# A recurrent-attention and MLP kernel: who issues the transfers, and a new written-out order

## The chip, the cores and the metric

The kernel runs on one core of a Trainium2 chip. A core has five engines with their own instruction queues: TensorE (PE in the profile), VectorE (DVE), ScalarE (ACT), GpSimd (POOL) and SyncE (SP), which here only issues transfers. Each queue is worked off strictly in order; an instruction that has to wait holds everything behind it on its engine. SyncE, ScalarE and GpSimd can issue DMA transfers, which sixteen DMA engines carry out. The metric is the device time of one launch in microseconds (us). Differences of less than about one per cent are hard to tell from no change.

## The reference

Two steps follow each other. The first is a recurrence over time with a per-channel decay, for 4 batches and 8 heads, 768 steps, head dimension 48:

```python
for t in range(S):
    kt, vt, rt, wt = (k[:, :, t], v[:, :, t], r[:, :, t], w[:, :, t])
    cur = np.einsum('bhd,bhe->bhde', u[None] * kt, vt)
    y[:, :, t] = np.einsum('bhd,bhde->bhe', rt, state + cur)
    state = wt[:, :, :, None] * state + np.einsum('bhd,bhe->bhde', kt, vt)
```

The second takes the result as 3072 rows of 384 numbers through an MLP with a softmax-gated activation and a normalisation:

```python
h = x @ w_in                              # 384 -> 1024
sm = softmax(h); solu = h * sm
ln = (solu - mean(solu)) / sqrt(var(solu) + 1e-6) * g_ln
out = ln @ w_out                          # 1024 -> 384
```

Inputs and outputs are float32: 18.9 MB of r, k, v and w, two weights of 1.6 MB each, 4.7 MB of output.

## The kernel before, in words

The time axis is cut into 6 chunks of 128 steps. A chunk of one batch, all 8 heads, is a unit; there are 24, numbered so that the four batches of a chunk follow each other (unit 4 is chunk 1 of batch 0). A unit is handled in matrix form. Its stages, by the names of the order:

- LW, LK, LR, LV load w, k, r, v of the unit (192 KB each, in rows of 192 bytes) into rings of 7 buffers. LU, LG, LI (three parts) and LO (two parts) load u, the gain g, w_in and w_out.
- lw takes the logarithm of w (ScalarE); cum sums it over time by two products (TensorE); ex takes exponentials in place (ScalarE); kp scales k and r by them (VectorE).
- krk and krr transpose the scaled k and r (TensorE), kr copies the result out of PSUM; M forms the scores (TensorE); m copies them, masked (VectorE, letter d) or unmasked (ScalarE, letter a), in which case sel masks them on GpSimd.
- p, q, dg, dv form the bonus term with u: p = k r, q = p u, dv = v dg on GpSimd, the row sum dg on VectorE. vb casts v.
- Y multiplies scores and v and adds the state's part; with the letter i it also adds dv by a product, otherwise y adds dv while copying on VectorE. S, et and st carry the state to the next chunk.
- X transposes y, xT copies it, H is the first MLP product (24 matmuls), e its exponential (ScalarE), he = h e (VectorE), hq its square. Oa and Ob are the two halves of the output product with the scaled weight w2, together with the sums for mean and variance. sq, qm, lv make the scale, o writes the scaled output, out stores it.
- Once per launch: wi casts w_in, gw scales w_out by g into w2 (eight pieces), mn and mc form the mean over rows of w2 and ce adds it (eight pieces: "centring"). Oa of unit 0 needs the centred pieces 0 to 3.
- us and uc spread u over the partitions by a product with a row of ones, gs and gc bring g into columns. hot issues n dummy products of 512 columns whose result is not used.

The order of all this work is written out by hand in ORDER: one word per stage, with the unit's number and, after the dot, a PSUM slot, the engine that does a copy (a ScalarE, d VectorE, p GpSimd) or, for loads, the queue that issues it (s SyncE, a ScalarE). The loop at the end of the kernel walks through the words, and the class InOrder ties each engine's instructions to that order, so no scheduler moves them. Before the loop stand the constants: masks, identities and the zero columns, on GpSimd and VectorE.

In the built program the transfers issued by SyncE and ScalarE share eight completion counters in turn. A transfer therefore waits, on its issuing engine, until the one eight places earlier in that turn has landed, besides waiting until its buffer is free.

Of the kernel before, what the change touches and what calls it, by code (L numbers as in the profile page):

```python
# [8 lines left out]
F32 = mybir.dt.float32  # L9
# [12 lines left out]
LW0.a LK0.s LU0.a LR0.s LW1.a LW2.s hot4.s3 LG0.s LK1.s lw0 LV0.a cum0.b0 LR1.s us0.s0 ex0 hot2.s3 uc0 lw1 LV1.s  # L22
p0 kp0 LW3.a LK2.a LR2.s krk0.s3 q0 krr0 cum1.b1 kr0.a hot2.s2 LV2.s LK3.a M0.b0 LR3.s p1 gs0.s1 ex1 m0.d
hot3.s3 LI1.s lw2 q1 dg0 cum2.b0 lw3 hot2.s3 kp1 vb0.p LI0.a S0.s2 dv0 vb1.a dg1 hot1.s3 ex2 Y0.is0 et0 LV3.a
cum3.b1 LI2.s p2 kp2 krk1.s3 gc0 LO0.s ex3 st0 LW4.s krk2.s1 q2 krr1 LO1.s krr2 kp3 kr1.a hot3.s2 dv1 LK4.s
kr2.d y0.a p3 M1.b0 LK5.a S1.s2 dg2 krk3.s3 vb2.a m1.d krr3 et1 wi0.a S2.s0 wi1.p M2.b1 st1 X0.s1 kr3.a m2.d
Y1.is2 LR4.s wi2.p et2 y1.a M3.b0 xT0.d LV4.a X1.s3 q3 m3.d H0.b1 dv2 gw1.a dg3 gw2.d e0 Y2.is2 LW5.s xT1.d
gw3.p st2 H1.b0 y2.a he0 lw4 gw0.a X2.s1 LR5.s e1 gw7.d cum4.b1 gw4.d hot2.s3 gw6.d gw5.d ex4 he1 vb3.p mn0.s3
LW6.s LV5.a dv3 xT2.a LK6.s kp4 S3.s0 mc0 Y3.is2 LR6.s lw5 ce6.d krk4.s1 ce3.d hq0.a cum5.b0 ce4.d krr4 ce2.d
H2.b1 ce7.d ex5 LW7.s ce1.d ce5.d ce0.d y3.a LK7.s p4 kp5 et3 Oa0.s3 lw6 e2 LR7.s kr4.d p5 krk5.s2 cum6.b0 st3  # L30
hq1.a Ob0 vb4.p he2 LW8.s q4 krr5 ex6 S4.s1 LK8.s kr5.d sq0 M4.b1 lw7 Oa1.s0 kp6 et4 m4.a LR8.s X3.s2 qm0 st4
vb5.p M5.b0 xT3.a cum7.b1 dg4 sel4 lv0 krk6.s1 LV6.s Ob1 m5.d ex7 LW9.s dv4 lw8 S5.s2 kp7 o0.a krr6 LK9.s p6
cum8.b0 sq1 et5 Y4.ns3 kr6.d ex8 H3.b1 q5 LV7.s y4.d hq2.a kp8 q6 LR9.s krk7.s1 e3 X4.s3 st5 LW10.s vb6.p M6.b0
krr7 xT4.d Oa2.s2 dg5 m6.a LK10.s qm1 kr7.d dv5 krk8.s3 lv1 Ob2 he3 out0 sel6 o1.a lw9 M7.b0 out1 dg6 S6.s1 sq2
m7.a LV8.s hq3.d krr8 cum9.b1 LR10.s Y5.ns0 vb7.p qm2 kr8.d lv2 H4.b0 p7 LW11.s et6 y5.d ex9 st6 p8 lw10 kp9
LV9.s X5.s3 S7.s0 e4 Oa3.s1 q7 o2.d vb8.a he4 out2 cum10.b1 dv6 xT5.a krk9.s2 et7 LK11.s ex10 Y6.ns3 q8 krr9 st7
LV10.s H5.b0 hq4.a kp10 sel7 LR11.s kr9.a y6.d M8.b1 dg7 LW12.s S8.s0 lw11 m8.d Ob3 dv7 et8 e5 LV11.s vb9.p
krk10.s3 st8 X6.s2 LK12.s p9 M9.b1 he5 xT6.a Y7.ns0 sq3 m9.a krr10 LR12.s S9.s2 dg8 cum11.b0 et9 LW13.s y7.d
H6.b1 lw12 dv8 ex11 kr10.d LK13.s p10 qm3 lv3 kp11 Oa4.s0 LR13.s e6 q9 st9 X7.s3 cum12.b0 LW14.s xT7.a Ob4 he6
p11 ex12 LV12.s krk11.s2 sel9 sq4 Y8.ns3 o3.a kp12 H7.b1 hq5.a out3 vb10.p qm4 y8.d q10 LK14.s lv4 dg9 M10.b0 e7  # L40
Oa5.s1 LR14.s m10.d vb11.p q11 o4.a krr11 LW15.s X8.s3 lw13 dg10 Ob5 p12 xT8.a out4 he7 kr11.a S10.s0 dv9 S11.s3
LV13.s dg11 sq5 hq6.a Y9.ns2 vb12.p qm5 cum13.b0 y9.d dv10 LK15.s H8.b1 et10 ex13 st10 LR15.s et11 lw14 kp13
Oa6.s2 LW16.s e8 hq7.d krk12.s0 lw15 M11.b0 p13 st11 LK16.s Ob6 lv5 he8 o5.a q12 krr12 m11.a Y10.ns3 out5 kr12.d
krk13.s1 cum14.b1 LR16.s y10.d sq6 krr13 sel11 ex14 cum15.b0 LW17.s kr13.d Oa7.s0 ex15 qm6 LV14.s kp14 p14
Y11.ns3 lw16 X9.s1 Ob7 kp15 lv6 dv11 LK17.s vb13.a xT9.d p15 o6.a M12.b1 y11.d M13.b0 m12.a X10.s1 out6 m13.d
krk14.s2 q13 S12.s3 LR17.s hq8.a krr14 H9.b1 dg12 LV15.s vb14.p xT10.d sq7 q14 et12 qm7 st12 LW18.s lv7 krk15.s1
dg13 e9 X11.s3 sel12 H10.b0 o7.d kr14.a out7 he9 dv12 LK18.s Y12.ns0 xT11.a p16 krr15 LR18.s Oa8.s2 e10 y12.d
kr15.d q15 LV16.s cum16.b1 he10 S13.s0 ex16 dv13 Ob8 LV17.s et13 kp16 q16 X12.s3 LW19.s Y13.ns1 sq8 xT12.a st13
M14.b0 vb15.p M15.b1 LK19.s m14.a y13.d krk16.s3 S14.s0 hq9.d krr16 LR19.s m15.a S15.s1 p17 qm8 kr16.d H11.b0
LW20.s et14 dg14 lv8 sel14 st14 et15 LK20.s dg15 H12.b1 e11 vb16.p o8.d sel15 st15 out8 lw17 Oa9.s3 he11 LV18.s  # L50
e12 vb17.p dv14 S16.s0 LV19.s hq10.a he12 Ob9 dv15 LR20.s et16 cum17.b0 st16 q17 Y14.ns2 LV20.s ex17 X13.s1
y14.d M16.b1 sq9 Oa10.s0 lw18 kp17 LW21.s m16.a Y15.ns2 qm9 xT13.d LK21.s cum18.b0 hq11.d lv9 krk17.s1 lw19
H13.b1 LR21.s o9.d p18 vb18.a dg16 ex18 LV21.s y15.d dv16 krr17 e13 Ob10 kp18 LW22.s sel16 X14.s3 hq12.a kr17.d
S17.s2 LK22.s cum19.b0 q18 he13 Oa11.s1 xT14.a LR22.s ex19 p19 X15.s3 lw20 M17.b1 out9 xT15.d Ob11 sq10 kp19
vb20.p m17.a LW23.s q19 Y16.ns3 qm10 dg17 et17 vb19.a cum20.b0 p20 LV22.s y16.d lv10 H14.b1 dg18 sq11 ex20 sel17
LK23.s st17 lw21 o10.d LR23.s Oa12.s3 e14 kp20 dv17 krk18.s2 Ob12 out10 hq13.a p21 qm11 he14 krk19.s0 LV23.s
lv11 krr18 q20 cum21.b0 sq12 o11.d krr19 ex21 H15.b1 p22 qm12 kr18.d out11 lv12 kr19.d vb21.p Oa13.s1 dv18 kp21
e15 X16.s2 o12.d Y17.ns0 xT16.a M18.b0 hq14.a y17.d out12 krk20.s3 Ob13 he15 lw22 X17.s0 m18.a krk21.s2 xT17.d
krr20 cum22.b1 dg19 krr21 sq13 sel18 ex22 qm13 S18.s0 dg20 H16.b0 kr20.d hq15.a q21 kr21.d lv13 kp22 Oa14.s3
dv19 e16 dv20 M19.b1 et18 Y18.ns2 he16 m19.a Ob14 lw23 sel19 y18.d M20.b1 sq14 M21.b0 o13.d Oa15.s2 m21.a st18  # L60
out13 m20.d krk22.s1 X18.s0 cum23.b0 xT18.a krr22 Ob15 ex23 hq16.d vb22.p dg21 kr22.a Y19.ns0 q22 kp23 H17.b1
vb23.a dv21 qm14 sq15 y19.d lv14 Y20.ns1 e17 p23 o14.d H18.b0 dg22 out14 sel21 qm15 y20.d lv15 krk23.s0 he17 e18
Oa16.s3 dv22 krr23 o15.a he18 q23 Ob16 kr23.a out15 X19.s1 M22.b1 xT19.d M23.b0 hq17.d X20.s2 S19.s0 xT20.a
hq18.d Oa17.s1 m22.a dg23 Y21.ns2 et19 m23.a sel22 st19 H19.b1 sq16 sel23 qm16 y21.d lv16 Oa18.s0 e19 dv23
X21.s2 Ob17 he19 H20.b0 sq17 o16.d xT21.d out16 Y22.ns3 qm17 e20 Y23.ns2 y22.d Ob18 y23.d hq19.a he20 H21.b1
lv17 o17.d X22.s3 Oa19.s2 e21 out17 xT22.d hq20.d X23.s1 sq18 H22.b0 he21 xT23.d Ob19 qm18 hq21.d e22 H23.b1
sq19 lv18 qm19 he22 Oa20.s3 e23 o18.d hq22.d Oa21.s1 out18 lv19 he23 Ob20 o19.d Ob21 sq20 hq23.d out19 Oa22.s0
sq21 qm20 qm21 lv20 Oa23.s2 lv21 o20.d o21.d out20 Ob22 out21 Ob23 sq22 qm22 lv22 sq23 qm23 o22.d lv23 out22
o23.a out23
# [27 lines left out]
def kernel(  # L97
# [14 lines left out]
    C = 128  # L112
# [20 lines left out]
    def bank(shape, dtype, slot, name):  # L133
# [15 lines left out]
    dve.memset(warm, 0.0)  # L149
    uti_neg = consts.tile([C, C], BF16)  # L150
    pool.memset(uti_neg, -1.0)
    pool.affine_select(out=uti_neg, in_=uti_neg, compare_op=ALU.is_ge, fill=0.0, base=0,
                       pattern=[[1, C]], channel_multiplier=-1)
    uts = consts.tile([C, C], BF16)
    pool.memset(uts, 1.0)
    pool.affine_select(out=uts, in_=uts, compare_op=ALU.is_gt, fill=0.0, base=0,
                       pattern=[[1, C]], channel_multiplier=-1)
    ident_f = consts.tile([C, C], F32)
    pool.memset(ident_f, 0.0)
    pool.affine_select(out=ident_f, in_=ident_f, compare_op=ALU.not_equal, fill=1.0, base=0,  # L160
                       pattern=[[-1, C]], channel_multiplier=1)
    ident = consts.tile([C, C], BF16)
    pool.tensor_copy(out=ident, in_=ident_f)

    halves = consts.tile([C, C], BF16)
    pool.memset(halves, 0.0)
    pool.memset(halves[0:2, :], 1.0)
    pool.affine_select(out=halves[0:2, :], in_=halves[0:2, :], compare_op=ALU.is_ge, fill=0.0, base=0,
                       pattern=[[1, C]], channel_multiplier=-64)
    pool.affine_select(out=halves[0:2, :], in_=halves[0:2, :], compare_op=ALU.is_gt, fill=0.0, base=64,  # L170
                       pattern=[[-1, C]], channel_multiplier=64)
    off_blocks = consts.tile([C, HP, 2], BF16)
    pool.memset(off_blocks, 0.0)
    pool.memset(off_blocks[0:2], -30000.0)
    pool.affine_select(out=off_blocks[0:2], in_=off_blocks[0:2], compare_op=ALU.not_equal, fill=0.0, base=0,
                       pattern=[[0, HP], [-1, 2]], channel_multiplier=1)

    one_col = consts.tile([C, 2], BF16)
    dve.memset(one_col, 1.0)
    inv_col = consts.tile([C, 1], BF16)  # L180
    dve.memset(inv_col, 1.0 / RDF)
    ones_row = consts.tile([1, C], F32)
    dve.memset(ones_row, 1.0)

    lw_t = ring("lw", NLW, [C, H, 64], BF16)
    kp_t = ring("kp", NKP, [C, 2, H, 64], BF16)
    for j in range(max(NLW, NKP)):
        if j < NLW:
            dve.memset(lw_t[j][:, :, D:], 0.0)
# [366 lines left out]
```

The softmax here doesn't subtract the row's maximum and nothing guards it: scores larger than these inputs give would overflow.

## Time and profile before

| | us |
|---|---|
| median of 3 runs (lowest, highest) | 152.22 (151.28, 153.02) |
| the profiled execution, its time | 153.27 |
| its span in the profile | 151.6 |
| TensorE busy | 137.2 (91%) |
| VectorE busy | 127.9 (84%) |
| ScalarE busy | 117.9 (78%) |
| GpSimd busy | 94.9 (63%) |

The granted TensorE clock is 0.994. The page has a line of digits per engine, one for each fortieth of the span: the busy share in tenths, 9 for nine tenths or more. The chain of work lists, from the last instruction back, what released each step; its rows are start, length, engine. The groups give the mean length of one instruction. A row of waits reads: who waited, for whom, us in total, how often, longest. TensorE's lengths overlap, since matmuls are pipelined; the distance from start to start tells what one costs.

Only SyncE and ScalarE issue transfers: 12 of ScalarE's are w of units 0, 1 and 3, k of units 2, 3 and 5, v of units 0, 3, 4 and 5, u, and one part of w_in. The mean time from issue to landing of a load is near 4 us.

### The profile page before, as it was taken

To read this page: it belongs to the slowest core of one execution; us is meant where nothing else is said; L and a number is where in the kernel's file an instruction comes from. 1 tells how busy PE (TensorE), PEld (TensorE's weight loads), DVE (VectorE), ACT (ScalarE), POOL (GpSimd) and SP (SyncE) were. 2 spreads that over 40 slices of the span, in tenths; PEclk is the share of its full clock that TensorE was granted. 3 is DMA by queue.
4 is the path that set the end of the run, shared out by engine and by line. 5 is a ranking of instruction groups with operands and counts; after the bars stand their busy time and mean duration, and the time that the engine had idled before them with its cause. 6 is when DMAs were issued, how large, how long until landed. Compare 5 with 4: busy or idle time off the path is not lost.

```text
span 151.6 us, 5258 instructions
## 1 busy us (share of the span) xinstructions
PE 137.2 (91%) x2156; PEld 106.6 (70%) x2158; DVE 127.9 (84%) x235; ACT 117.9 (78%) x238; POOL 94.9 (63%) x127
## 2 busy tenths in 40 slices
PE   4799787879999997999988999999999999999980
PEld 1145566467788776888777797878887888889650
DVE  5209797999999996999976999999998998688940
ACT  3465766599999997999798688999898997484442
POOL 7484993531879859993849999299847682500000
PEclk9999999999999999999999999999999999999997
DMA  5999999999983999989699999898950111011142
GB/s 110 259 257 334 405 335 255 178 210 188 224 179 121 229 217 193 215 176 241 142 243 208 230 175 232 162 230 193 248 164 6 52 56 52 4 52 56 52 160 104
DMA packets 104825, 27.08 MB, mean 179 GB/s; under 512 B 100313, under 2 KB 104418, under 8 KB 104802
## 3 DMA queue, kind: packets, MB, share of 16 engines
q1 hardware_dynamic: 94256, 24.26, 69.6%
q10 hardware_dynamic: 10546, 2.49, 7.3%
q8 instruction: 17, 0.28, 0.7%
q14 instruction: 6, 0.05, 0.1%
HBM read 22.03 MB, written 4.72 MB: 176 GB/s over the span
## 4 chain that ended last, share of the span: by engine, by line
PE 54%; DMA 12%; SPq 10%; DVE 8%; ACT 6%; POOL 4%; issue 4%; ACTq 0%; POOLq 0%
PE o_ps L89 22%; PE h_ps L89 13%; SPq L89 10%; DMA w_in<-in_w_dram 6%; PE kr_ps L89 4%; PE y_ps L89 4%; DMA kr_in<-in_r_dram 4%; PE s_ps L89 3%; PE cum_ps L89 3%; PE m_ps L89 3%; DMA v_in<-in_v_dram 3%; PE x_ps L89 2%; DVE he L89 1%; POOL m L89 1%; DVE w L89 1%
## 5 line engine op out<-in xcount | busy, mean ns | idle before, releaser
L89 PE MATMUL o_ps<-w,he 128*128 128x385 bf16 x192 | 45.7, 325 | 0.1
L89 PE MATMUL h_ps<-xT,win_sb 128*128 128x128 bf16 x576 | 35.9, 219 | 0.3 <-DVE xT L89 0.3
L89 PEld LDWEIGHTS <-win_sb 128*128 128x128 bf16 x576 | 33.0, 98 | 0.9 <-issue 0.4
L89 PE MATMUL o_ps<-inv_col,e 128*128 128x1 bf16 x192 | 31.7, 165 | 0.0
L89 DVE TENSOR_TENSOR he<-h_ps,e 128x1024 bf16<-128x1024 f32 x24 | 29.1, 1216 | 2.7 <-ACT e L89 2.5
L89 PE MATMUL o_ps<-one_col,hq 128*128 128x1 bf16 x192 | 31.3, 163 | 0.0
L89 ACT ACTIVATE e<-h_ps 128x1024 bf16<-128x1024 f32 x24 | 24.5, 1020 | 4.7 <-PE h_ps L89 4.6
L89 DVE TENSOR_TENSOR kp<-cum_ps,kr_in 128x768 bf16<-128x768 f32 x24 | 22.7, 948 | 5.9 <-ACT cum_ps L89 5.6
L89 PEld LDWEIGHTS <-hq 128*128 128x128 bf16 x192 | 18.5, 96 | 12.8
L89 POOL TENSOR_TENSOR p<-kr_in 128x384 bf16<-128x384 f32 x24 | 24.4, 1018 | 3.7 <-DMA kr_in<-in_r_dram 3.6
L89 POOL TENSOR_TENSOR dv<-vb,dg 128x384 bf16<-128x384 bf16 x24 | 19.8, 830 | 9.6 <-DVE dg L89 7.4
L89 POOL TENSOR_SCALAR_AFFINE_SELECT m<-m 128x1024 bf16<-128x1024 bf16 x15 | 16.8, 1120 | 13.4 <-ACT sq L89 5.8
L89 POOL TENSOR_TENSOR q<-p,u_bc 128x384 bf16<-128x384 bf16 x24 | 21.8, 911 | 1.9 <-ACT u_bc L89 1.7
L89 PEld LDWEIGHTS <-kp 128*128 128x128 bf16 x272 | 17.4, 98 | 6.0 <-DVE kp L89 2.1
L89 ACT ACTIVATE cum_ps<-cum_ps 128x768 f32<-128x768 f32 x24 | 19.2, 802 | 3.0 <-PE cum_ps L89 2.9
L89 PE MATMUL kr_ps<-ident,kp 128*128 128x128 bf16 x192 | 18.0, 222 | 2.3 <-ACT gr L89 0.8
L89 PEld LDWEIGHTS <-he 128*128 128x128 bf16 x192 | 18.4, 96 | 0.9
L89 PEld LDWEIGHTS <-e 128*128 128x128 bf16 x192 | 18.4, 96 | 0.5 <-issue 0.2
L89 ACT ACTIVATE lw<-w_in 128x384 bf16<-128x384 f32 x24 | 12.4, 523 | 4.1 <-DMA w_in<-in_w_dram 4.1
L89 ACT CAST m<-m_ps 128x1024 bf16<-128x1024 f32 x15 | 15.0, 1013 | 0.7 <-PE m_ps L89 0.6
L89 DVE TENSOR_TENSOR m<-m_ps,keep 128x1024 bf16<-128x1024 f32 x9 | 10.9, 1215 | 4.2 <-PE m_ps L89 4.2
L89 ACT ACTIVATE hq<-he 128x1024 bf16<-128x1024 bf16 x13 | 13.7, 1057 | 0.0
(82 smaller groups left out, 262.5 us busy)
## 6 DMA issues: line engine op xcount, KB each, us to landing
kr_in<-in_r_dram SPq DMA_DIRECT2D x24, 192.0 KB, 4.3
out_dram<-o SPq DMA_DIRECT2D x24, 192.0 KB, 3.2
kr_in<-in_k_dram SPq DMA_DIRECT2D x21, 192.0 KB, 3.5
w_in<-in_w_dram SPq DMA_DIRECT2D x21, 192.0 KB, 4.2
v_in<-in_v_dram SPq DMA_DIRECT2D x20, 192.0 KB, 4.1
wout_f<-in_moe_w_out_dram SPq DMA_DIRECT2D x2, 768.0 KB, 7.7
win_f<-in_moe_w_in_dram SPq DMA_DIRECT2D x2, 512.0 KB, 5.1
v_in<-in_v_dram ACTq DMA_DIRECT2D x4, 192.0 KB, 4.2
```

The lines of the kernel that those rows point to most:

```text
L89: made = make(*args, **kwargs)
```

## The change

Five things are changed together.

1. ScalarE issues only k and r of unit 0, r of unit 1, and v of units 0 and 1. All other loads of units are SyncE's.
2. GpSimd gets a queue for transfers (letter p): the first two parts of w_in, g, both parts of w_out, and 13 of the 24 stores (units 0 to 7, 10, 16, 17, 22, 23). The third part of w_in is SyncE's. The first part of w_in is issued before the constants are made, which for that became a stage of their own (pc).
3. u is cast to bf16 (stage ur, on VectorE), and so is the row of ones, before the product that spreads it.
4. The dummy rows grow from 19 products to 33; the first run has 8 instead of 4.
5. ORDER is new throughout. Four H stand ahead of the first Oa instead of three; nine more of the scaled outputs are ScalarE's (17 instead of 8), three more kr copies and two more masked score copies VectorE's; all w_in casts are ScalarE's; two centrings are GpSimd's.

```diff
 ORDER = """
-LW0.a LK0.s LU0.a LR0.s LW1.a LW2.s hot4.s3 LG0.s LK1.s lw0 LV0.a cum0.b0 LR1.s us0.s0 ex0 hot2.s3 uc0 lw1 LV1.s
-p0 kp0 LW3.a LK2.a LR2.s krk0.s3 q0 krr0 cum1.b1 kr0.a hot2.s2 LV2.s LK3.a M0.b0 LR3.s p1 gs0.s1 ex1 m0.d
...
+LI0.p pc0 LW0.s LK0.a LR0.a LU0.s hot8.s3 LW1.s LW2.s LK1.s lw0 LR2.s LR1.a LG0.p cum0.b0 hot2.s3 ex0 ur0 p0
+LV0.a kp0 us0.s0 hot3.s3 LK2.s lw1 uc0 cum1.b1 krk0.s3 LW3.s q0 LV1.a krr0 ex1 hot6.s2 LK3.s p1 kr0.a kp1 LV2.s
+LI1.p lw2 dg0 M0.b0 wi0.a cum2.b1 m0.d LO0.p LR3.s krk1.s2 hot6.s3 vb0.a q1 LW4.s lw3 dv0 ex2 cum3.b0 gs0.s1
...
-    ones_row = consts.tile([1, C], F32)
+    ones_row = consts.tile([1, C], BF16)
...
+    def constants(i, x):
+        dve.memset(warm, 0.0)
+        pool.memset(uti_neg, -1.0)
...
+    u_b = consts.tile([1, DM], BF16)
...
-    queue = {"s": sp, "a": act}
+    queue = {"s": sp, "a": act, "p": pool}
...
+    def round_u(i, x):
+        dve.tensor_copy(out=u_b, in_=u_row)
...
-        pe.matmul(ps["u"], lhsT=ones_row, rhs=u_row, start=True, stop=True)
+        pe.matmul(ps["u"], lhsT=ones_row, rhs=u_b, start=True, stop=True)
...
     def store(i, x):
         c, b = units[i]
-        sp.dma_start(out=out[b * S + c * C:b * S + (c + 1) * C, :], in_=o_t[i % NWK])
+        queue[x or "s"].dma_start(out=out[b * S + c * C:b * S + (c + 1) * C, :], in_=o_t[i % NWK])
...
     stages = dict(
+        pc=constants,
...
+        ur=round_u, us=spread_u, uc=copy_u, gs=turn_g, gc=copy_g, wi=cast_w_in, gw=gain, mn=column_mean, mc=copy_mean,
```

## The prediction

> **What bounds the kernel now.** I read the forty slices first, then the chain of work that ended last, then TensorE's own waits, then the waits in the built program.
>
> ```profile
> PE   4799787879999997999988999999999999999980
> POOL 7484993531879859993849999299847682500000
> DMA  5999999999983999989699999898950111011142
> GB/s 110 259 257 334 405 335 255 178 210 188 224 179 121 229 217 193 215 176 241 142 243 208 230 175 232 162 230 193 248 164 6 52 56 52 4 52 56 52 160 104
> ```
>
> A slice is 3.79 us. TensorE (PE) is full from slice ten on; before that it has holes, while the DMA engines are full. The last third needs hardly any DMA. So there are two stages: a head limited by arrivals and by the other engines, and a body limited by TensorE. The chain shows where the head ends:
>
> ```profile
> 20.62 4.20 SPq L89
> 24.87 1.16 SPq L89
> 26.07 3.79 DMA w_in<-in_w_dram
> 29.88 0.37 ACTq L89
> 30.43 0.25 issue
> 30.67 0.49 ACT mean_sb L89
> 31.27 0.45 issue
> 31.72 1.97 DVE w L89 x7
> 33.73 0.99 PE o_ps L89 x12
> ```
>
> SyncE holds the load of w5 for 4.20 us: each load waits on a counter shared with the load eight places earlier, here a half of w_out. ScalarE stands behind its own v5 load in the same way (29.88) and so copies the mean late; VectorE centres w2, and the first output product, Oa0, runs at 33.73.
>
> Now a ledger for TensorE. The chain's back-to-back rows give its cost per unit: H 1.34, Oa and Ob 0.83 each, Y 0.39, M 0.33, cum 0.33, krk and krr 0.47, X 0.18, S 0.46. Over 24 units (S for 20), plus 1.8 for mean, u and g, that is 123.8 us. Of it, 15.4 stand ahead of Oa0 in the order. So the head loses 33.73 - 15.4 = **18.3**. The other 108.4 take until 146.4, where the chain leaves TensorE: 112.7, so **4.3** lost in the body. From there to the end of the span **5.2**. 123.8 + 18.3 + 4.3 + 5.2 = 151.6, the span; the profiled execution took 153.27, 1.05 above the median of 152.22, so I carry differences over to the median.
>
> TensorE's waits from 33.7 us to 146.4 are few:
>
> ```profile
> PE cum_ps L89 <- DVE kp L89: 0.8, 1, 0.8
> PE y_ps L89 <- POOL m L89: 0.7, 1, 0.7
> PE kr_ps L89 <- ACT o L89: 0.7, 1, 0.7
> PE y_ps L89 <- ACT xT L89: 0.2, 1, 0.2
> ```
>
> They sum to 2.4 us; the body can give back little more. In that stretch VectorE is busy 104.1 of 112.7 us, ScalarE 95.5, GpSimd 73.2.
>
> **The change, part by part.**
>
> *More work ahead of Oa0.* The new order puts 19.6 us of TensorE work before Oa0 (four H instead of three, transposes of seven units instead of five), 4.2 more than 15.4. If Oa0 stayed at 33.73, the gain would be 4.2. It will not stay: VectorE has more to do first. Before, it works from the mask of unit 0 (11.53) to the last gain of w2 (26.69 + 2.15 = 28.84), idle some 2.5 us in between (0.92 and 1.11 of it waiting for ScalarE). The new order adds two kr copies (0.60 each, by starts), one kp (0.87), one dg (0.46) and one gain (0.53): 3.1 us. Idle time may absorb from none to 2.5 of it, so the mean's product, which ended at 29.55, ends between 30.1 and 32.6; I take 32.1, since the added kp waits for r4, which lands late. After it TensorE still has 4.6 us before Oa0, giving 36.7. VectorE by itself agrees: last gain at 31.4, then ahead of the piece ce0 that Oa0 reads: st 0.46, two kp 1.74, he 1.14, kr 0.60, five ce 1.35, in sum 5.3. So Oa0 at 36.7, lag 17.1: **-1.2**. Bounds: -3.0 (mean at 30.1) to +1.5 (LI2, fifteenth on SyncE, holds H0 3 us).
>
> *ScalarE's queue.* Seven loads leave it. Its idle time before v4, v5 and the g copy (2.48, 1.87, 1.42 us) goes, and the mean is copied at once; this is in the sum above. What remains are the waits of v0 and v1 behind w2 and r2, with u's copy and ex1 queued after them: at most the 1.2 us by which ScalarE already idles at 8.2, inside the bounds. All loads from unit 2 on are now SyncE's.
>
> *Weights and stores on GpSimd.* Five loads (two of w_in, g, two of w_out) and 13 stores. No GpSimd-issued transfer is in this trace. Its price p on GpSimd is at least 0; nearest rows: ScalarE's issues, 0.37, SyncE's single stores, 0.58 to 0.96, and SyncE's second half of w_out, 1.98, which I take as upper end. I use p = 1.0, near the stores. Compute moves little: two fewer masks (-2.2) and w_in casts (-2.1), two more v casts (+1.0) and centrings (+1.7 at the dv row's 0.83). In the head GpSimd reaches dv4 at about 29 us with five issues; TensorE needs it only after the mean's product, so 2 to 3 us of cover. In the body the tight place is dv10: from ce1 (mean copied at 32.6, both centrings done 34.4) 27.8 us of rows and five stores, 62.2 + 5p, against y10 due at 36.7 + (50.9 - 19.6) = 68.0, plus 0.5 for y9 ahead of it on VectorE. So nothing is late up to p = 1.25. What stands behind such a store on GpSimd is dv, then y, X and H of that unit.
>
> The page "SBUF — State Buffer" of the Trainium skill (Who interferes with whom, and the summary) speaks against this part: descriptors of a GpSimd-issued DMA are made by GpSimd itself and wait while VectorE holds the shared port, 620 ns alone against some 3100 ns beside a copy. By these figures p would be 0.6 to 3.1, an estimate, and the upper end would cost some 9 us at dv10. Nothing in this trace shows it.
>
> *One queue instead of two.* From 8 to 12 us, with ScalarE's and SyncE's queues loading, 257 GB/s moved; from 28 to 32 and 32 to 36 us, with SyncE's nearly alone, 192 and 186. "DMA: Bandwidth & Descriptors" (Issuing engines are not separate DMA queues) says a second issuer saves only issue time; by that rule nothing is lost here and r6 lands two or three us sooner, an estimate that moves Oa0 by nothing. By the rows alone: 8.4 MB had moved by 32 us before, r6 stands 8.3 MB into the new order, so it lands near 31, in time for krk6 at 35.8.
>
> *u in bf16 and dummy rows.* The u product falls from two passes (1.64 us) to one, about the 0.48 of a cum row; the added cast on VectorE (0.35, as an xT copy) fits in its 3.44 us of idle time. Dummies go from 19 to 33 rows, 8 instead of 4 at the start. Rows step 0.43 us before 13 us and 0.21 after, so eight fill 1.25 to 4.7 and the speed may double earlier; unit 0's cum, transposes and scores would lose about 1.0 us. But GpSimd's first transfer competes with w0, k0 and r0 (0.5 MB, 1.5 us at 350 GB/s). I set them against each other, 0, bounds -1.0 to +1.5. If the speed doesn't double, the 25 later dummies cost up to 5 us of TensorE time, partly in gaps.
>
> *The body.* Nine scaled outputs go from VectorE (0.609) to ScalarE (0.576); with the other moves VectorE carries 2.8 us less, ScalarE 2.7 more, and both stay below TensorE. I let half of the 2.4 us of waits go: **-1.2**; bounds -2.4 to +4 (next rival).
>
> *The tail.* The last store is issued by GpSimd after o23: p = 1.0 instead of SyncE's 0.6: **+0.5**, bounds -0.6 (p = 0) to +1.4.
>
> Sum: -1.2 - 1.2 + 0.5, about **-2.0**: 151.3 for the profiled execution, **150.2** for the median.
>
> **Rivals.** (1) *GpSimd becomes the bound*, slower. For: it is nine tenths busy in many slices already, and its share in the body rises from 73 us by nine stores. Against: cover up to p = 1.25. At p = 2, dv10 is late by 3.7, and five head issues put up to 1.5 more before H1; with the gains of 2.0 kept that is 155, with the head's gain lost too 156.
> (2) *The gain stays in the head*: H0 or kp4 waits for single-queue loads, Oa0 reaches 38, the body keeps its 4.3: 152, no difference.
> (3) *Everything covers*: Oa0 at 34.9 (-3.0), body -2, tail 0: 147.3.
>
> **How the numbers follow.** Forecast 0.38, (3) 0.10, (2) 0.27, (1) 0.25. About 1% (1.5 us) is what a measurement here can tell from no change. The forecast lies just beyond it, so a small part of it counts as same: faster 0.45, same 0.28, slower 0.27. Range 147.3 to 155.5: it leaves out the worst of (1) and little below (3).
>
> **What would show it.** Right: Oa0 starts at 35 to 37.5, after the mean's product at 30 to 32.6; no ScalarE wait on a v load after 15 us; GpSimd's issues near 1 us; TensorE's waits after Oa0 below 3 us. Wrong: GpSimd rows over 1.25 us at stores, y waiting for dv in units 9 to 13, or dummy rows still 0.43 apart after 8 us. The step I trust least is p, then the arrival of r4 and LI2.

## The result, and the profile after

The changed kernel takes **162.12 us** (median of 4 runs, 161.60 to 163.34) against 152.42 for the kernel before on the same chip: 1.0658 times as long, 95% interval 1.0567 to 1.0749. Forecast were 150.2 us and a range up to 155.5. The profiled execution has a span of 160.0 us, 8.4 more than before. Ratios, here and below, leave disturbed executions out, so a median can lie somewhat above its ratio.

The forty slices of the page after (a slice is 4.0 us):

```profile
PE   6769977868599999999999959989999999999950
POOL 6859649949509988999999980849978533410011
PEclk9955999999999999999999978999999999999998
DMA  5999998999999899989999239797641101012032
GB/s 133 286 248 309 359 359 181 203 186 215 191 197 227 167 238 213 220 162 268 232 219 223 76 76 214 163 228 167 151 99 53 49 4 53 16 64 74 4 147 98
```

Three places differ from before. The granted TensorE clock drops to half in slices three and four. TensorE has holes until slice eleven, where before they ended with slice nine. And in the middle of the body the transfers fall to 76 GB/s for two slices, with a hole and a lower clock on TensorE.

The ledger of the prediction, taken from the new trace: the first output product, Oa0, starts at 42.61 with 19.56 us of work ahead of it, so the head loses **23.05** (18.3 before, +4.7). TensorE's last product ends at 154.3: the other 104.2 us of work took 111.7, so the body loses **7.5** (before, with the end of the last product at 147.2, 5.1; +2.4). The rest of the span is **5.7** (4.4 before, +1.3). The three differences are the 8.4. (The prediction cut the body of before at 146.4, which gave 4.3 and 5.2.)

The chain of work that ended last, in the head (start, length, what):

```profile
16.34 7.68 DMA kr_in<-in_r_dram
24.14 0.97 DVE kp L89
...
32.10 2.28 DVE w L89 x4
34.38 0.47 DVE st L89
...
39.62 2.87 DMA v_in<-in_v_dram
42.49 0.33 DVE w L89
```

The head now runs over r of unit 4, which lands 7.7 us after it could be issued, and then over VectorE: at 32.10 its gains of w2, at the end the centred pieces. The row ahead of the last one carries the name of a transfer, but VectorE was working then, on these pieces:

```profile
37.36 1.03 DVE L89 TENSOR_TENSOR w<-w,mean_sb 128x384 bf16<-128x384 bf16 x1
39.18 3.65 DVE L89 TENSOR_TENSOR w<-w,mean_sb 128x384 bf16<-128x384 bf16 x5
```

The groups of instructions say what was long (busy us and mean ns of one after the bar), two rows of the kernel before and then three of the changed one:

```profile
L89 DVE TENSOR_TENSOR hq<-he 128x1024 bf16<-128x1024 bf16 x11 | 8.2, 757 | 0.0
L89 DVE TENSOR_TENSOR w<-w,mean_sb 128x384 bf16<-128x384 bf16 x8 | 2.5, 380 | 0.4 <-ACT mean_sb L89 0.4
```

```profile
L89 DVE TENSOR_TENSOR hq<-he 128x1024 bf16<-128x1024 bf16 x10 | 11.5, 1150 | 0.1
L89 DVE TENSOR_TENSOR w<-w,mean_sb 128x384 bf16<-128x384 bf16 x6 | 4.7, 832 | 0.0
L89 POOL DMA_DIRECT2D out_dram<-o x13 | 7.5, 576 | 20.0 <-ACT sq L89 11.7 <-ACT o L89 7.4 <-DVE o L89 0.6
```

A centring piece took 832 ns on average where it took 380 before, an hq 1150 where it took 757. The stores that I feared take 0.58 us each on GpSimd.

How the head starts late is in ScalarE's timeline (ACTq is its issue of a transfer):

```profile
8.54 0.44 ACTq L89 DMA_DIRECT2D v_in<-in_v_dram  x1
9.02 0.52 ACT L89 ACTIVATE lw<-w_in 128x384 bf16<-128x384 f32 x1 [2.70 <-DMA w_in<-in_w_dram]
```

The issue of v0 was held until 8.54; behind it the second logarithm ran at 9.02 instead of 7.67. TensorE idled 2.65 us and then worked at the low clock. By stretches of four us (busy time of PE, PEld, DVE, ACT, POOL; granted clock, DMA share, GB/s):

```profile
8.00:12.00 4.00, 2.40 (x13) 1.50 (x13) 0.42 (x2) 2.13 (x4) 2.01 (x4) 0.60 1.24 248
12.00:16.00 4.00, 4.00 (x22) 1.73 (x21) 2.27 (x4) 3.54 (x7) 3.82 (x5) 0.55 1.20 309
```

The first scores, behind six dummy rows at that clock (2.76 us), started at 13.74 instead of 10.81.

In the body, TensorE has two long waits for VectorE; VectorE's timeline shows where the first is from, and GpSimd's stands beneath it:

```profile
PE x_ps L89 <- DVE o L89: 1.8, 1, 1.8
PE o_ps L89 <- DVE w L89: 1.3, 1, 1.3
```

```profile
90.27 2.94 DVE L89 TENSOR_TENSOR hq<-he 128x1024 bf16<-128x1024 bf16 x1
93.14 0.60 DVE L89 TENSOR_SCALAR o<-o_ps,rs 128x384 f32<-128x384 f32 x1
```

```profile
89.48 1.78 POOL L89 TENSOR_TENSOR q<-p,u_bc 128x384 bf16<-128x384 bf16 x2
91.22 1.00 POOL L89 TENSOR_TENSOR p<-kr_in 128x384 bf16<-128x384 f32 x1
92.16 1.41 POOL L89 CAST vb<-v_in 128x384 bf16<-128x384 f32 x2
```

The hq of unit 10, 0.68 us when alone, took 2.94 beside GpSimd's q, q, p and the beginning of its casts. Unit 8's output was scaled only after it, and the store of that output stood first in SyncE's line:

```profile
85.65 0.66 SPq L89 DMA_DIRECT2D w_in<-in_w_dram  x1
93.77 0.36 SPq L89 DMA_DIRECT2D out_dram<-o  x1
```

Nothing was loaded for the 7.5 us between the two rows; the stretch of the square is 2.3 of them, the rest is the store's place in the line. That is the hole in the transfers, and the lag of TensorE behind its ledger jumps there from 24.6 (hidden product of unit 11) to 27.8 (unit 12).

### The profile page after: what moved, and what is told of

Same layout as the page of the kernel before. It is cut to its first block, busy times and chain, and to the rows that moved or that the text cites. A ratio compares the mean times of both kernels' runs of the same rounds, so it can differ in the third digit from the quotient of the medians.

```text
span 160.0 us, 5313 instructions
## 1 busy us (share of the span) xinstructions
PE 141.0 (88%) x2169; PEld 109.0 (68%) x2172; DVE 133.9 (84%) x228; ACT 120.1 (75%) x244; POOL 106.6 (67%) x145
## 4 chain that ended last, share of the span: by engine, by line
PE 38%; DVE 20%; issue 11%; SPq 11%; DMA 8%; ACT 6%; POOL 2%; POOLq 0%; DVEq 0%
PE o_ps L89 12%; SPq L89 11%; PE h_ps L89 10%; DMA kr_in<-in_r_dram 5%; PE kr_ps L89 4%; DVE kp L89 3%; DVE hq L89 3%; DMA v_in<-in_v_dram 3%; PE s_ps L89 3%; PE y_ps L89 3%; PE m_ps L89 3%; PE cum_ps L89 2%; DVE he L89 2%; DVE w L89 2%; DVE dg L89 2%
## 5 line engine op out<-in xcount | busy, mean ns | idle before, releaser
L89 PE MATMUL h_ps<-xT,win_sb 128*128 128x128 bf16 x576 | 36.4, 220 | 0.3 <-ACT m L89 0.3
L89 POOL TENSOR_TENSOR dv<-vb,dg 128x384 bf16<-128x384 bf16 x24 | 20.6, 864 | 11.9 <-DVE dg L89 11.5
L89 POOL DMA_DIRECT2D out_dram<-o x13 | 7.5, 576 | 20.0 <-ACT sq L89 11.7
L89 POOL TENSOR_SCALAR_AFFINE_SELECT m<-m 128x1024 bf16<-128x1024 bf16 x13 | 15.1, 1159 | 3.1 <-ACT sq L89 3.0
L89 ACT ACTIVATE hq<-he 128x1024 bf16<-128x1024 bf16 x14 | 14.8, 1058 | 1.8 <-DVE he L89 1.8
L89 DVE TENSOR_TENSOR m<-m_ps,keep 128x1024 bf16<-128x1024 f32 x11 | 13.4, 1219 | 1.7 <-PE m_ps L89 1.6
```

The source lines that it names most:

```text
L89: made = make(*args, **kwargs)
```

## The experiments

Times are medians; the ratio is to the kernel before on the same chip, with its 95% interval. "Lag" is the start of a TensorE step minus the work ahead of it in the order. Of ORDER the edits show only the changed words with some neighbours; "..." marks what is left out.

### Which part: the order, the weights, the stores or the loads (e1 to e4)

The new order, with all that it put on GpSimd's queue given back to SyncE:

```diff
-LI0.p pc0 LW0.s LK0.a LR0.a
+pc0 LW0.s LK0.a LR0.a
...
-LI1.p lw2 dg0 M0.b0 wi0.a cum2.b1 m0.d LO0.p
+LI0.s LI1.s lw2 dg0 M0.b0 wi0.a cum2.b1 m0.d LO0.s
...
-kr7.d out0.p st5
+kr7.d out0.s st5
...
```

(likewise LG0, LO1 and the other twelve stores)

> The changed kernel with the five weight loads, g's load and the 13 stores issued by SyncE again (w_in's first third stands beside the second in the order). Theory A, the order: the loss of 9.7 us comes from where the new order puts work (v's first two loads on ScalarE ahead of the second log, TensorE's idle time and low clock after it, the sums of w2 and the products hq on VectorE beside GpSimd's reads). Then most of it stays: 157 to 162 us, the first output product still at 40 us or later, and only the end gets shorter by about 1 us. Theory B, the queues: the loss comes from transfers started by GpSimd (the weights crowd the unit loads, the stores take GpSimd's time). Then the time goes back to 151 to 154.5 us.

Measured: **160.89 us**, 1.0497 (1.0413 to 1.0582). Oa0 at 43.63, and from TensorE's end to the end of the span 4.5 us, as before the change. Both as theory A has it. The head is as bad by another route: w_in's first third comes later, ScalarE stands 4.96 us in line for its cast, and TensorE idles:

```profile
12.00:16.00 4.00, 0.86 (x4) 0.29 (x3) 0.10 (x1) 0.23 (x1) 0.00 (x0) 1.00 1.09 333
```

The old order with the weights on GpSimd's queue:

```diff
-LG0.s LI1.s LI0.a LI2.s LO0.s LO1.s
+LG0.p LI1.p LI0.p LI2.p LO0.p LO1.p
```

> The kernel before, with the three loads of w_in, the two of w_out and g's issued by GpSimd at the places they had in the order. Theory A (order): 151 to 153.5 us, the r of unit 4 lands within 1 us of before. Theory B (queues): the weights crowd the unit loads, r of unit 4 and w_in's last third land 2 us or more later, and the time is 154.5 to 158 us.

Measured: 160.69 us, 1.0406 (1.0343 to 1.0469). Theory A alone falls: this part costs the old order some 6 us by itself. Its two shortest executions took 158.9 us, a little more than theory B's 158; in the profiled one (163.4 us) Oa0 came at 40.90, 7.2 later.

The old order with the stores on GpSimd:

```diff
-krr7 xT4.d Oa2.s2 dg5 m6.a LK10.s qm1 kr7.d dv5 krk8.s3 lv1 Ob2 he3 out0
+krr7 xT4.d Oa2.s2 dg5 m6.a LK10.s qm1 kr7.d dv5 krk8.s3 lv1 Ob2 he3 out0.p
...
-sp.dma_start(out=out[b * S + c * C:b * S + (c + 1) * C, :], in_=o_t[i % NWK])
+queue[x or "s"].dma_start(out=out[b * S + c * C:b * S + (c + 1) * C, :], in_=o_t[i % NWK])
```

(likewise out1 to out7, out10, out16, out17, out22 and out23)

> The kernel before, with the 13 stores of the changed kernel issued by GpSimd. Six or seven of the body's stores cost GpSimd about 0.58 us each; GpSimd has slack. Theory A (order): 152 to 154 us, where up to 1.1 us is the end, since the last store then leaves through GpSimd's queue, and the body does not move by more than 0.5 us. Theory B (queues): the stores take GpSimd from the bonus products and the body is 2 us or more longer, 154.5 to 157 us.

Measured: **157.43 us**, 1.0307 (1.0260 to 1.0354), just above theory B's range. But Oa0 is unmoved (33.83), and GpSimd is not the bound. VectorE is busy 4.8 us more in sum, and one group holds that, its squares:

```profile
L89 DVE TENSOR_TENSOR hq<-he 128x1024 bf16<-128x1024 bf16 x11 | 13.3, 1220 | 0.0
```

Two of the eleven took 3.12 and 3.94 us (0.68 when alone). This gave theory C: a VectorE product with two inputs in SBUF is stretched while GpSimd works, and the stores shift GpSimd's work beside it.

The old order with ScalarE's loads from unit 2 on, and w_in's first third, on SyncE:

```diff
-LW3.a LK2.a LK3.a LI0.a LV3.a LK5.a LV4.a LV5.a
+LW3.s LK2.s LK3.s LI0.s LV3.s LK5.s LV4.s LV5.s
```

> The kernel before, with the eight loads that ScalarE issued for units 2 to 5 and w_in's first third issued by SyncE, as in the changed kernel. ScalarE is freed of eight issues; SyncE's line of loads in the head gets longer. Theory A (order): 150.5 to 153 us. Theory B in its other form (one queue for nearly all unit loads is too slow): the r and w loads of units 3 to 5 land 2 us or more later, and the time is 154.5 to 158 us.

Measured: **155.29 us**, 1.0164 (1.0114 to 1.0213). Oa0 at 36.20, 2.5 later, and nothing else moved. Unit 5's logarithm waits for its w until 32.94; in the kernel before, w5 had landed at 29.86. One line for nearly all unit loads costs 2.5 us here. The four costs (8, 6, 5 and 2.5 us) sum to twice the 9.7 of the whole change: they overlap, and none is a share of it.

### The stretched products (f1, f2, g4, g5)

```diff
-hq10.d
+hq10.a
...
-out22.p out23.p
+out22.s out23.s
```

> The changed kernel with the product hq of unit 10 on ScalarE instead of VectorE, where it took 2.94 us beside three GpSimd instructions, and the stores of units 22 and 23 by SyncE. The two edits show in different places. Theory C (a VectorE product with two SBUF inputs is stretched by GpSimd's reads, and this one made the jump of 3 us at 91 to 96 us): TensorE's end comes 2 to 3 us earlier and the stretch of idle time with the lower clock at 92 to 100 us goes. Rival (the stall there is that of the stores and loads themselves): TensorE's end moves by less than 0.7 us. The end after TensorE's last product falls by about 1 us in both. Time by C 158 to 159.5 us, by the rival 160.3 to 161.5 us.

Measured: **159.51 us**, 1.0435 (1.0336 to 1.0534), 2.6 us less. The lag's jump between the hidden products of units 11 and 12 falls from 3.2 to 0.6, and the end after TensorE from 5.7 to 4.5. TensorE's end itself came only 0.4 earlier, because Oa0 in this execution came at 44.16; counted from Oa0, the body is 1.9 us shorter. The transfers still fall to 68 GB/s from 92 to 96 us, but TensorE is busy for 3.67 of these 4 us (2.21 in the changed kernel). Theory C for the body, and the last stores for the end.

```diff
-hq3.d
+hq3.a
...
-hq9.d
+hq9.a
```

> The kernel before with the 13 stores on GpSimd, and the products hq of units 3 and 9, which took 3.12 and 3.94 us on VectorE in that run, on ScalarE at 1.06 us each. Theory C (the stores cost through the stretch: they delay GpSimd, whose instructions then stand back to back beside hq): TensorE's end goes back from 150.2 to 147.3 to 148.2 us, and with the longer end the time is 154 to 155.3 us. Rival (GpSimd's own 0.58 us for each store is what binds): TensorE's end stays within 0.7 us and the time at 156.7 to 158 us.

Measured: **152.83 us**, 1.0013 (0.9977 to 1.0048): all of the 4.6 us that the stores had cost is gone, with the stores still on GpSimd. TensorE ends at 145.77, earlier than before the change. The squares left on VectorE:

```profile
L89 DVE TENSOR_TENSOR hq<-he 128x1024 bf16<-128x1024 bf16 x9 | 6.3, 705 | 0.0
```

So the two squares were enough to take back the stores' price. They are not shown to be all of it: the time is better than theory C's 154 to 155.3, and TensorE ends 1.4 us earlier than in the kernel before, so part may be a gain that the move of two squares to ScalarE brings without the stores. The kernel before with that move alone was not run.

Centring with one SBUF input, on top of f1:

```diff
-(dve if x == "d" else pool).tensor_add(out=w2[:, f, :DM], in0=w2[:, f, :DM], in1=mean_sb)
+(dve if x == "d" else pool).tensor_add(out=w2[:, f, :DM], in0=w2[:, f, :DM], in1=ps["mean"] if x == "d" else mean_sb)
...
-LW8.s X4.s2 ce6.d krk6.s1 ce7.d H3.b1 e2 ce5.d ce0.d LK8.s ce4.d lw7
+LW8.s ce6.d krk6.s1 ce7.d H3.b1 e2 ce5.d ce0.d LK8.s ce4.d X4.s2 lw7
```

> The kernel with hq of unit 10 on ScalarE and the last two stores by SyncE (159.5 us), with VectorE's six additions of the mean to w2 reading the mean from PSUM instead of its copy in SBUF, so that they have one SBUF input; the transposes of unit 4's y, which take the mean's bank, stand after them. Five of the six took 4.70 us together in that run beside GpSimd, and 0.35 us alone. Theory C (a second SBUF input is what stretches them): each takes 0.5 to 0.6 us whatever GpSimd does, and the first output product comes 1 to 2 us earlier; time 157.5 to 158.7 us. Rival (they are slow for another reason, or the wait is covered): the five still take 4 us or more, or the first output product moves by less than 0.5 us; time 159 to 160.2 us.

Five pieces in f1, and the same five here, from VectorE's timelines:

```profile
40.39 4.70 DVE L89 TENSOR_TENSOR w<-w,mean_sb 128x384 bf16<-128x384 bf16 x5
```

```profile
41.32 2.39 DVE L89 TENSOR_TENSOR w<-w,mean_ps 128x384 bf16<-128x384 bf16 x5
```

They take 0.48 us each, beside GpSimd too. Measured: 158.55 us, 1.0426 (1.0349 to 1.0502), 1.0 less than f1 by medians, though the ratios alone would not tell the two apart. Oa0 did not move (44.15). In this execution the mean's product ended at 37.73, 0.7 later than in f1, and from there to Oa0 it took 6.4 us instead of 7.2; the edit itself puts X4 ahead of Oa0 behind all six pieces, and TensorE waited 0.6 us there for the last one. By the hidden product of unit 4 the lag is 24.7 against 26.0 in f1. The size of the instructions is as theory C has it; the place of the gain is not.

A candidate to beat both: f2 with the stores of units 22 and 23 by SyncE.

```diff
-out22.p out23.p
+out22 out23
```

> The kernel before with hq of units 3 and 9 on ScalarE and 11 of the 13 stores on GpSimd, those of units 22 and 23 left to SyncE. Its sister with all 13 on GpSimd took 152.8 us, with TensorE's end 1.4 us earlier than before and an end 0.9 us longer. If the longer end is that of GpSimd's last stores, this takes 151.4 to 152.1 us and is faster than before by 0.5 to 0.9%; if the end stays, 152.5 to 153.2 us.

Measured: 152.20 us in 12 runs, 1.0048 (1.0007 to 1.0088). Median and ratio point in different directions by half a per cent; it is no faster version. The end is 0.7 us shorter than f2's, but Oa0 came 1.3 later.

### The head: single loads and waits (f3, f4, g1, g2)

```diff
-LV0.a LV1.a
+LV0.s LV1.s
```

> The changed kernel with the first two loads of v issued by SyncE instead of ScalarE. Theory D (ScalarE's held issue of v0 delays the second log, TensorE then stands idle, its clock falls, and the dummies at the low clock hold the first scores): the second log starts at 7.5 to 8 us instead of 9.0, the clock stays full at 8 to 16 us, the first scores come 2 to 3 us earlier and the first output product 1.5 to 3 us earlier; time 159 to 160.6 us. Rival (the hold is handed on: SyncE's line of loads is held in its place and r of unit 4 and w_in's last third land as late): the first output product moves by less than 0.8 us; time 161.3 to 162.8 us.

Measured: **164.72 us**, 1.0723 (1.0617 to 1.0828). All of theory D's first steps came: the second logarithm at 7.96, full clock until 20 us, the first scores at 10.83. Then the gain was lost; whether more than the gain is not clear, since the interval overlaps that of the changed kernel. In the profiled execution (165.3 us; the four went from 162.8 to 165.3) all engines stood still for 4 us, waiting for r of unit 3 and w of unit 4, and the low clock was paid there (whether the shorter executions stood still as long is not known):

```profile
20.00:24.00 4.00, 0.00 (x0) 0.00 (x0) 0.00 (x0) 0.00 (x0) 0.00 (x0) 0.58 0.74 198
```

The rival's sentence, that the hold is handed on, fits; the time lies above its 161.3 to 162.8.

The old order with u in bf16:

```diff
+ur0
 us0.s0
...
-rhs=u_row
+rhs=u_b
```

> The kernel before with u rounded to bf16 on VectorE and spread by a bf16 product, in the old place. In the kernel before the fp32 product takes 1.64 us of TensorE from 5.6 us on, and the copy of u on ScalarE waits 0.78 us for it ahead of the second log. If that stood on the path to the first output product, the time falls by 0.7 to 1.3 us, to 151.3 to 152 us; if the weights' arrival covers it, it stays at 152.3 to 153.2 us.

Measured: **154.82 us**, 1.0172 (1.0086 to 1.0258): slower, which neither side expected. The product with its cast takes less (the product 0.49 us instead of 1.64), and the first scores start 0.84 earlier, at 9.97. But ScalarE's first gain now runs at 26.01, where it ran at 23.99 before, behind v4's issue and w_out's landing, and Oa0 comes at 35.87, 2.1 later. ScalarE, being earlier, issued v3 at 13.46 instead of 15.45, ahead of other loads. That this is the reason is argued from the timeline, not tried.

The version of f1 with the loads in the sequence and on the queues of the kernel before:

```diff
-LI0.p pc0 LW0.s LK0.a LR0.a LU0.s hot8.s3 LW1.s LW2.s LK1.s lw0 LR2.s LR1.a LG0.p cum0.b0
+pc0 LW0.a LK0.s LU0.a LR0.s hot8.s3 LW1.a LW2.s LG0.s lw0 LK1.s LV0.a LR1.s cum0.b0
...
-LI1.p lw2 dg0 M0.b0 wi0.a cum2.b1 m0.d LO0.p LR3.s krk1.s2
+LI1.s lw2 dg0 M0.b0 cum2.b1 m0.d LI0.a LV3.a krk1.s2
...
-krk3.s3 dv1 wi1.a krr3
+krk3.s3 dv1 wi0.a wi1.a krr3
```

> The kernel with hq of unit 10 on ScalarE and the last two stores by SyncE (159.5 us), in which every load now stands in the sequence and on the queue that the kernel before had, weights too, laid into the places where the new order has a load; the cast of w_in's first third goes next to that of the second. The new order of the arithmetic stays, and the stores in the body stay on GpSimd. Theory L (the transfers are the bound of the head: their engines are busy without a gap from 2 to 27 us, so the sequence in which loads go out decides when r of unit 4, the weights and with them the first output product can come): the first output product goes from 44.2 to 37 to 39.5 us and the time to 153 to 156 us. Rival (the new order of the arithmetic itself makes the head late): the first output product stays at 41 us or later, time 157 to 160 us.

Measured: 168.47 us (164.97 to 169.52), the largest median of all, without a ratio; its shortest execution is longer than any of f1's. In the profiled one (167.7 us) Oa0 stands at 46.38. The loads' old sequence is no cure: unit 4's scaled k now waits for its r until 27.02, as late as in the kernel before (26.97), but the new order has that step ahead of the first hidden product, which comes at 29.86.

Only w_in's first third and its cast later:

```diff
-LI0.p pc0 LW0.s LK0.a
+pc0 LW0.s LK0.a
...
-LI1.p lw2 dg0 M0.b0 wi0.a cum2.b1
+LI0.p LI1.p lw2 dg0 M0.b0 cum2.b1
...
-krk3.s3 dv1 wi1.a krr3
+krk3.s3 dv1 wi0.a wi1.a krr3
```

> The kernel with hq of unit 10 on ScalarE and the last two stores by SyncE (159.5 us), with one thing moved: the load of w_in's first third goes from the first place of all to a place beside the second third, still on GpSimd, and its cast next to the second third's. It had moved 0.53 MB in the first 10 us, in which the units' loads moved 1.64 MB against 2.01 before. Theory L: those transfers come back to the units' loads, the second log starts 1.5 to 2 us earlier, and the first output product 1.5 to 3 us earlier; time 156.5 to 158.2 us. Rival (the hold of SyncE's later loads by the weights on GpSimd's queue stays, so that the gain is lost by 24 us): the first output product moves by less than 1 us; time 158.6 to 160 us.

Measured: 160.89 us, 1.0596 (1.0507 to 1.0684): no clear gain. SyncE was held 5.13 us at 12.28 ahead of unit 4's w, and VectorE then waited 6.14 us for r of unit 3.

### The head as a whole (h1 to h4, i1, i2)

Both orders with 0.9 instead of 3.1 MB of weights:

```diff
-part = slice(j * KF // 2, (j + 1) * KF // 2)
+part = slice(j * KF // 2, j * KF // 2 + 1)
...
-in_=win_f[:, j, :]
+in_=win_f[:, 0, :]
...
-in_=wout_f[:, f, :]
+in_=wout_f[:, f // (KF // 2) * (KF // 2), :]
```

> The kernel before with fewer bytes of weights: only the first third of w_in is loaded (at the place of the second) and used three times, and of each half of w_out one quarter, used four times; 0.9 instead of 3.1 MB. The output is that of other weights; the arithmetic and its order are the same. At the 430 GB/s at which weights passed, 2.2 MB are some 5 us of the transfers. Theory L (the transfers bound the head): the first output product comes 2 to 4.5 us earlier than 33.7, time 148.5 to 151 us. Rival (it is bound by the arithmetic ahead of it): less than 1 us earlier, time 152 to 153 us.

> The new order with the sums of w2 read from PSUM, hq of unit 10 on ScalarE and the last two stores by SyncE (158.6 us), with the same fewer bytes of weights, 0.9 instead of 3.1 MB, the kept third of w_in at the first place of all. Theory L: the stall that stood at 8 to 12 us or at 24 us shrinks, the first output product comes 4 to 6.5 us earlier than 44.2, time 152.5 to 155 us, and the distance to the kernel before with the same weights falls from 5.7 us to 4 us or less. Rival (the order of the arithmetic by itself): the first output product gains no more than in the kernel before, and the distance stays at 5 us or more.

Measured: the old order **151.57 us**, 0.9887 (0.9833 to 0.9941), 1.5 less; Oa0 stayed at 33.70, so theory L's expectation for it fails: what it gained all lies behind Oa0, and the old order hides most of its weights ahead of it. The new order **153.89 us**, 1.0128 (1.0038 to 1.0217), 4.7 less than g4 with all weights; Oa0 at 39.30, lag 19.7 (24.6 in g4), as theory L has it. The distance of the two orders falls from 5.7 us to 2.3. What the weights took can be read from the transfers between 10 and 28 us, by queue (q1 is SyncE's, q0 GpSimd's: packets, MB, share of the 16 engines), g4 and then h2:

```profile
q1 hardware_dynamic: 11516, 2.68, 66.6%
q0 software_dynamic: 528, 2.10, 28.5%
```

```profile
q1 hardware_dynamic: 17985, 3.40, 95.0%
q0 software_dynamic: 128, 0.39, 5.6%
```

and what TensorE made of it in one stretch, again g4 and then h2:

```profile
24.00:28.00 4.00, 1.44 (x26) 1.38 (x26) 2.37 (x3) 1.55 (x4) 2.39 (x4) 0.92 0.84 203
```

```profile
24.00:28.00 4.00, 4.00 (x77) 3.14 (x74) 3.97 (x7) 3.92 (x9) 3.83 (x6) 1.00 1.08 213
```

The transfers' engines are full in both. Of SyncE's 2.68 MB in g4, 0.52 are w_in's last third, so 2.16 MB of unit loads passed, against 3.40 in h2. In h2 the stall at 9 us and the low clock after it are still there (first scores at 13.59), and yet the lag is nearly the old one: in that version the stall and its dummies are not the bulk of the head's loss.

```diff
-kp2 vb1.a ex3 LO1.p kr1.d LR4.s
+kp2 vb1.a ex3 kr1.d LR4.s
...
-X0.s0 p3 LV3.s
+X0.s0 p3 LO1.p LV3.s
```

> The same version of the new order (158.6 us) with one load moved: the second half of w_out, 0.77 MB, is issued by GpSimd after the bonus product of unit 3, behind r of unit 4 and w_in's last third instead of ahead of them. Theory L: r of unit 4 and w_in's last third land 1 to 2 us earlier, the first hidden product comes 1 to 2 us earlier, time 156.8 to 157.9 us. Rival (the place of a weight load makes no difference, or the delayed w_out takes the gain back): 158 to 159.5 us.

```diff
-hot6.s2
+hot2.s2
```

> The same version of the new order (158.6 us) with two instead of six dummy products ahead of the first scores, where each took 0.43 us at the low clock. The first scores come 1.2 to 1.8 us earlier. Theory D (that delay, handed on by every engine, is part of the loss): the first output product comes 1 us or more earlier, time 157 to 157.9 us. Theory L (the loads of units 3 and 4 are awaited later anyway): it is given back, the first output product moves by less than 0.6 us, time 158 to 159.2 us. Shorter dummies may also leave TensorE idle for longer and the clock low for longer; then the time is above 159.2 us.

Measured: h3 157.02 us, 1.0302 (1.0207 to 1.0398); h4 157.26 us, 1.0287 (1.0165 to 1.0409). Both are 1.3 to 1.5 us below g4 by medians, but the intervals overlap g4's, so each only leans towards its theory. The profiled executions, the longest of each (160.8 and 158.1 us), do not settle it: in h3's the first hidden product came at 29.55, not earlier; in h4's the first scores came 1.1 us earlier, Oa0 0.6 (43.58).

```diff
-krr3 cum4.b0 q3 xT0.d LV4.s kr3.d ex4 Y1.is0 M2.b1 st0 LW5.s y1.a p4 kp4 m2.a
+krr3 q3 xT0.d LV4.s kr3.d Y1.is0 M2.b1 st0 LW5.s y1.a m2.a
...
-wi2.a q4 S2.s2 m3.d krk4.s0 krr4 sel2 et2 H0.b1 kr4.a dg3 st1 dv2 gw2.a xT1.d LR5.s
+wi2.a S2.s2 m3.d sel2 et2 H0.b1 dg3 st1 dv2 gw2.a xT1.d cum4.b0 ex4 p4 kp4 q4 krk4.s0 krr4 kr4.a LR5.s
```

> The new order with the sums of w2 from PSUM, hq of unit 10 on ScalarE and the last two stores by SyncE (158.6 us), in which unit 4's cumulative sum, exponentials, bonus products, scaled k and r, transposes and their copy stand behind the first hidden product and unit 1's transposed copy, as in the kernel before, instead of ahead of them. Theory L (VectorE waited 2.5 us and GpSimd 4.1 us for r of unit 4, with unit 3's and the first hidden product's work behind them in line): the first hidden product comes 0.5 to 2 us earlier, until w_in's last third binds it, and the time is 156.5 to 158 us. Rival (the total of the head's work and transfers binds, not this place): the time stays at 158 to 159.5 us.

and with w_in's last third and w_out's second half exchanged:

```diff
-kp2 vb1.a ex3 LO1.p kr1.d LR4.s krk2.s0 gc0 krr2 dg1 Y0.is3 q2 kr2.d LI2.s S0.s2 y0.a
+kp2 vb1.a ex3 LI2.p kr1.d LR4.s krk2.s0 gc0 krr2 dg1 Y0.is3 q2 kr2.d S0.s2 y0.a
...
-X0.s0 p3 LV3.s
+X0.s0 p3 LO1.p LV3.s
```

> The same, and w_in's last third is issued by GpSimd at the place of w_out's second half, which goes behind unit 3's bonus product. Theory L: the first hidden product no longer waits for either, it comes 3 to 4 us earlier than 28.0, and the time is 154.5 to 156 us. Rival: as in the sister, 158 to 159.5 us; or w_out's second half is now what the gains wait for, and the first output product moves by less than 1 us while the first hidden product comes earlier, 157 to 159 us.

Measured: i2 160.74 us, 1.0492 (1.0410 to 1.0574); i1 **158.23 us**, 1.0346 (1.0260 to 1.0432). The first hidden product did come earlier, at 24.91 and 23.92 instead of 28.0. Oa0 came at 45.21 and 43.21 (44.15 in g4). The waits moved behind the first hidden product: in i1 the second one starts at 33.6. So it is not this place either: i1 lies in its rival's range, i2 above both.

## Why the prediction was wrong

**The head (-1.2 predicted, +4.7 measured).** The step that failed is "More work ahead of Oa0", with its bounds of -3.0 to +1.5. It counted VectorE's added rows at the durations of before and let only "LI2" hold something up; "One queue instead of two" beside it moved Oa0 "by nothing". Two terms went wrong by about the same amount. The mean's product ended at 34.8, not at 32.1: +2.7. From there to Oa0 it took 7.8 us, not 4.6: +3.2.

The first is the transfers. The prediction took "8.4 MB had moved by 32 us" and asked whether the last load of a line arrives in time. In the trace w_in's second third and w_out's halves were issued between 11.9 and 16.8 us, r of unit 4 only at 18.9, and it landed at 24.0; the new order wants units 3 and 4 ahead of its first hidden product, and units 5 and 6 ahead of Oa0. So the sequence in which loads go out is likely what matters, but no run shows that: with the old sequence (g1) the kernel had the largest median of all. The full transfers' engines cost the new order nearly one for one: 2.2 MB less gave 4.7 us, against 1.5 in the old order. By an estimate from the 391 to 437 GB/s that moved while weights passed in the kernel before, 2.2 MB are 5.0 to 5.6 us. With them gone the mean's product ended at 32.87 (h2), near the 32.1 predicted. Shown are this total, and that the queue matters: weights on GpSimd's queue cost the old order 6 us (e2), one line of unit loads 2.5 (e4). Moves of single loads or steps did not gain clearly (f3, g1, g2, h3, i1, i2). Which transfer does it in the new order stays open, if any single one does, and so do the last 2.3 us between h1 and h2. The Trainium skill's "DMA: Bandwidth & Descriptors" (Issuing engines are not separate DMA queues) says that a second issuer only saves issue time; e2 and e4 changed hardly more than the issuer and cost 6 and 2.5 us, so for a saturated stage here the measurement decides against the use I made of the rule. Rival (2) named the wait that came, kp4 for r of unit 4 (0.90 us, at 24.14), but with Oa0 at 38 not its size.

The second is the stretch of the centring pieces, "five ce 1.35" in the prediction. In the changed kernel the five ahead of Oa0, the one at 37.36 and the first four from 39.18 on, took some 4.3 us, which is 3.0 of the 3.2. g4 showed that the second SBUF input is what makes them long: with one in PSUM five took 2.39. That this brings Oa0 forward is not shown, since Oa0 stayed where it was in g4.

**ScalarE's queue.** The wait of v0 was named, "at most the 1.2 us", and was 1.35 at the second logarithm. But the step stopped there. Behind it TensorE's clock fell and dummies at 0.43 us held the first scores until 13.74, 2.9 us late. That outweighs the 0 (up to +1.5) which the step "u in bf16 and dummy rows" had set. The warning it named, dummies 0.43 apart after 8 us, came. In h2, with fewer weights, this delay can be at most 1.4 us of Oa0's lag (19.7 against 18.3); f3, which took it away, was no faster; f4 shows that starting earlier need not help at all.

**Weights and stores on GpSimd.** The price p was the step I trusted least, and it was harmless: 0.58 us for a store, 0.78 for a half of w_out, far from the threshold of 1.25; no y waited for a dv. The rival that ended on the slower side got the sign right by a mechanism that did not occur.

**The body (-1.2 predicted, +2.4 measured, inside its bounds of -2.4 to +4).** The bound was right for a wrong reason. The time was lost at one square, through an output, to a store at the head of SyncE's line. Moving that one square to ScalarE took most of the jump away (f1, 3.2 to 0.6); moving two took back as much as the stores had cost in the old order (f2). The Trainium skill's "SBUF — State Buffer" (Who interferes with whom, and the summary) states this: a VectorE instruction with two SBUF inputs contends with a GpSimd instruction that reads SBUF, and the second to issue is blocked until the first finishes. The runs agree, and go further: 0.68 us alone, 2.94, 3.12 and 3.94 beside several GpSimd instructions in a row, so such an instruction was held by more than one of them. The prediction drew on that page for the descriptors alone.

**The tail (+0.5 predicted, +1.3 measured, inside its bounds).** The cause, the last stores on GpSimd, was right: given back to SyncE they returned 1.1 us (f1). The price put on it was not: predicted was a longer issue, p = 1.0 instead of 0.6, but the last issue took 0.54 us. The time lies behind it, 3.1 us from its end to the end of the span against 2.5 before, and ahead of it: 2.0 us from TensorE's end to its start, where 1.9 reached to its end before. That the measured value fell inside the bounds was luck.

The sum: -2.0 predicted, +8.4 measured.

## What to carry to other kernels

When a change moves work on GpSimd, look for VectorE instructions with two SBUF inputs in the same stretch, and price them at the length of the GpSimd run that they may stand in, not at their usual duration; send them to ScalarE, or read one input from PSUM. In a stage where the transfers are full, count the bytes that the order needs ahead of each step, in the sequence in which they go out, and ask what an earlier start sends out earlier. A gain at the start of such a stage need not be a gain at its end: f3, f4, i1 and i2 each moved an early step forward, and in none did Oa0 gain clearly.

## What the runs showed of the hardware that I had not expected

- One square of 128x1024 bf16 with two SBUF inputs: 0.68 us alone, up to 3.94 beside a run of GpSimd instructions. A piece of 128x384: 0.38 us on average in the kernel before, five of them 4.70 beside GpSimd (f1), and 2.39 with one input in PSUM (g4).
- After 2.65 us without work on TensorE the granted clock stood at 0.60 and 0.55 in the eight us from 8 to 16; without that gap it was 1.00 there (f3). The length alone does not decide: in e2's profiled execution a gap of 2.79 us (15.50 to 18.29) left it at 1.00 up to 24 us.
- A smaller product for u (0.49 instead of 1.64 us) made the old order 1.7% slower.
- A transfer issued by GpSimd cost it 0.54 to 0.80 us, even for 768 KB, beside stores while VectorE was some nine tenths busy in the body, and beside the 768 KB halves of w_out while it was busy for little more than half of the time (2.27 of the 4 us from 12 to 16).
